# Attention and MLP in one kernel: layer-normed rows transposed by the DMA queue, token rows cast on the way in

## The chip, the cores and the metric

The kernel runs on one core of a Trainium2 chip. The metric is the device time of one execution in microseconds (us), and lower is better. Five engines work side by side, each through its own instructions in order: TensorE (PE in the profile), VectorE (DVE), ScalarE (ACT), GpSimd (POOL) and SyncE (SP, which here only issues transfers). TensorE's weight loads have a row of their own (PEld). They meet at semaphores: an instruction that needs another engine's result, or a landed transfer, waits, and everything behind it on its engine waits with it.

## What is computed

For 8 batches of 8 heads, with 576 tokens and 64 columns a head:

```python
scores = scale * q @ k.T                       # per head, 576 x 576
bias   = -(cum[:, None] - cum[None, :])        # cum = cumsum(max(s, 0))
scores = where(causal, -1e9, scores + minimum(bias, 0))
x      = softmax(scores) @ v                   # heads side by side: 576 x 512 a batch
xn     = (x - mean) / sqrt(var + 1e-6) * g_ln
out    = x + relu(xn @ w_ch1) @ w_ch2          # 512 -> 2048 -> 512
```

Inputs and outputs are float32; the kernel multiplies in bf16.

## The kernel before

**Order.** The order of all instructions is written by hand. A long plan, in words, covers the start (head numbers n up to 17; n counts the 64 heads, batch b = n // 8, head h = n % 8). From n = 18 on, one loop step handles one head. A step first calls `pre(n)`, which issues transfers and casts for later heads; then it puts on TensorE the head's scores, one "unit" of the MLP, on even heads the small last corner of the scores for two heads (`scores_d`), another unit, the product with v of the head two steps earlier (`pv_next`), and some more units.

**Attention of one head.** `scores` multiplies keys and queries into three banks of 512 columns; the bias is four extra rows of the operands (68 rows instead of 64). ScalarE takes the exponential of each bank into `er` (L345). From head 10 on, GpSimd zeroes the masked triangles in `er` with two `affine_select` instructions a head (L354) and one for each two heads (L384). Two steps later `pv` multiplies with v (L412) and `pv_norm` divides on VectorE (L424 to L433). `er` has four slots, used in turn.

**MLP of one batch.** It lies in a queue of 32 units of four matmuls each (128x512): 16 units for the first product (`mlp1`, L520, its relu on ScalarE or VectorE) and 16 for the second (`mlp2`, L538; every fourth ends in `yo`, L547 on VectorE, and an output transfer on SP, L565). The units are spread over eight steps. The queue of batch b-1 is filled at head 3 of batch b, after what was left of the older one has run. The last 64 tokens of two batches are put together into one tile (`xm`, transposed into `xTm`), which is worked off at the very end (`mixed_units`).

**Layer norm.** After the last head of a batch, `pv_next` computes mean and variance and then, one after the other, the 4 (even batches) or 5 (odd batches) tiles `xn` of 128x512 in bf16 on VectorE (L469, L487), and `ln_rstd` (one instruction on VectorE, one on GpSimd, L466). In heads 2 and 3 of the next batch, `ln_tr` transposes each tile on TensorE: four 128x128 transposes into PSUM (L505), and one copy to `xT` or `xTm` by VectorE (ScalarE for batches 1 and 7; L115, L113).

**Keys and queries.** They are needed transposed, with head columns on partitions. Groups `gam` of four heads (two a batch) have one of two homes, `kq0` and `kq1`, in turn. For groups 5 to 15 a group takes this way, for each of five token tiles t: `ld_rows` loads 128 token rows of k and q in float32 (two transfers on SP, L174); `cast_rows` casts them on GpSimd to bf16 (L186) and copies the four bias columns beside them (L187), into one of four row buffers taken in turn; `tr_rows` issues a DMA transpose on SP (L196), which writes the group's home. The row buffers lie in the unused `kq2`. In step n = 4 gam + m the loads are issued at m = -6, -5, -4, the casts at -5, -4, -3 and the transposes at -4, -3, all in `pre(n)`, so ahead of that step's masks on GpSimd.

**Values.** `ld_cast_v` loads v for a batch in five transfers issued by GpSimd that cast on the way (L164): two at 4 steps and three at 3 steps before the batch begins.

**Queues.** SP carries, in program order, the row loads, the row transposes and the outputs; GpSimd's own queue carries v.

Of the kernel before, what the change touches and what calls it, by code (L numbers as in the profile page):

```python
# [15 lines left out]
P = 128  # L16
# [3 lines left out]
def kernel(  # L20
# [11 lines left out]
    nc = tc.nc  # L32
    B, H, S, D = q.shape
# [5 lines left out]
    NF = S // P  # L39
    NT = NF + 1  # L40
    TL = S - NF * P
    SP = NT * P
    BH = B * H
# [4 lines left out]
    NG = BH // G  # L48
    NPE = 5
    NM = 10  # L50
    NR = 4
    KT = 96
    QT = 6
    QP = S // QT
# [34 lines left out]
    def home(gam):  # L89
# [5 lines left out]
        spare[:, i * 2 * G * P : (i + 1) * 2 * G * P].rearrange(  # L95
            "p (u h c) -> p u h c", u=2, h=G
        )
        for i in range(NR)
    ]

    er = const.tile([P, 4, EW], BF16, name="er")
# [9 lines left out]
    def copy_on(eng, out, in_):  # L111
        if eng == "act":
            nc.scalar.copy(out=out, in_=in_)  # L113
        elif eng == "dve":
            nc.vector.tensor_copy(out=out, in_=in_)  # L115
        else:
            nc.gpsimd.tensor_copy(out=out, in_=in_)
# [44 lines left out]
    def ld_cast_v(b, t):  # L162
        pn = P if t < NF else TL
        nc.gpsimd.dma_start(  # L164
            out=v_bf[b % 2][:pn, t, :, 0:D],
            in_=v[b, :, t * P : t * P + pn, :].rearrange("h s d -> s h d"),
        )

    def ld_rows(gam, t):
        pn = P if t < NF else TL  # L170
        b, h0 = gam // 2, (gam % 2) * G
        tmp = stage.tile([P, 2, G, D], F32, name="rowtmp", tag="st")
        for u, src in enumerate((k, q)):
            nc.sync.dma_start(  # L174
                out=tmp[0:pn, u],
                in_=src[b, h0 : h0 + G, t * P : t * P + pn, :].rearrange("h s d -> s h d"),
            )
        loaded["rows", gam, t] = tmp

    turn = [0]  # L180

    def cast_rows(gam, t):
        pn = P if t < NF else TL
        r = rows[turn[0] % NR]
        turn[0] += 1
        nc.gpsimd.tensor_copy(out=r[0:pn, :, :, 0:D], in_=loaded.pop(("rows", gam, t))[0:pn])  # L186
        nc.gpsimd.tensor_copy(  # L187
            out=r[0:pn, :, :, D:KA], in_=cT[0:pn, t, :, gam * G : (gam + 1) * G, :]
        )
        ready["rows", gam, t] = r  # L190

    def tr_rows(gam, t):
        pn = P if t < NF else TL
        r = ready.pop(("rows", gam, t))
        o = t * 2 * G * P
        nc.sync.dma_start_transpose(  # L196
            out=kq[home(gam)]
            .rearrange("p u h s -> p (u h s)")[:, o : o + 2 * G * pn]
            .rearrange("p (h s) -> p h s", s=pn),
            in_=r[0:pn].rearrange("p u h c -> p (u h c)"),  # L200
        )

    w1_r = moe_w_ch1.rearrange("(kd p) dh -> p kd dh", p=P)
# [160 lines left out]
    def scores_d(b, j):  # L364
        u0 = (2 * j) % 4
        pe_mask = b * H + 2 * j < NM
        ed = er[0:TL, u0 : u0 + 2, OD : OD + TL]
        d = ps_t.tile([P, 2, TL], F32, name="sd", tag="tr")
        for u in range(2):
            nc.tensor.matmul(  # L370
                d[:, u, :],
                lhsT=k_cols(b, 2 * j + u, NF),
                rhs=q_cols(b, 2 * j + u, NF * P, S)[0][2],
                start=True,
                stop=not pe_mask,
            )
            if pe_mask:
                nc.tensor.matmul(
                    d[:, u, :], lhsT=ident, rhs=maskT[:, 0:TL], start=False, stop=True
                )  # L380
        nc.scalar.activation(out=ed, in_=d[0:TL], func=ACT.Exp, scale=scale)
        if pe_mask:
            return
        nc.gpsimd.affine_select(  # L384
            out=ed,
            in_=ed,
            compare_op=ALU.is_ge,
            fill=0.0,
            base=0,
            pattern=[[0, 2], [1, TL]],  # L390
            channel_multiplier=-1,
        )
# [78 lines left out]
    def ln_xn(b, t):  # L471
        tiles = x_tiles(b)
        if t >= len(tiles):
            return
        if b == 0:
            nc.vector.tensor_scalar(
                out=mean0[:, t : t + 1],
                in0=sum0[:, t, 0:1],
                scalar1=sum0[:, t, 1:2],
                scalar2=1.0 / Dm,  # L480
                op0=ALU.add,
                op1=ALU.mult,
            )
        else:
            ln_aggr(b, t)
        xn = xnp.tile([P, Dm], BF16, name="xn", tag="xn")
        nc.vector.scalar_tensor_tensor(  # L487
            out=xn,
            in0=tiles[t],
            scalar=mvs[b][:, t, 0:1] if b > 0 else mean0[:, t : t + 1],  # L490
            in1=gb,
            op0=ALU.subtract,
            op1=ALU.mult,
        )
        xns[b, t] = xn
        if b > 0 and t == len(tiles) - 1:
            ln_rstd(b)

    def ln_tr(b, t, eng="dve"):
        if (b, t) not in xns:  # L500
            return
        xn = xns.pop((b, t))
        tr = ps_t.tile([P, KD, P], BF16, name="trx", tag="tr")
        for kd in range(KD):
            nc.tensor.transpose(tr[:, kd, :], xn[:, kd * P : (kd + 1) * P], ident)  # L505
        if eng is None:
            return tr
        if t < NF:
            dst = xTs[b][:, :, t * P : (t + 1) * P]
        else:  # L510
            dst = xTm[:, :, (b // 2) * P : (b // 2 + 1) * P]
        copy_on(eng, dst, tr)

    first_unit = [False]

# [63 lines left out]
    def run_units(n, dve_first=False):  # L579
        for i in range(n):  # L580
            if queue:
                first_unit[0] = dve_first and i == 0
                queue.pop(0)()
# [251 lines left out]
    def pre(n):  # L835
        if n == 14:
            for r in rows:
                nc.gpsimd.memset(r[:, :, :, KA:P], 0.0)
        if n in PAIR_LOADS:
            ld_cast_pair(PAIR_LOADS[n])  # L840
        if n in (11, 12):
            ld_w2(n - 9)
        if n in (8, 9):
            aug(n - 5, nc.sync)
        for gam in range(NPE, NG):
            m = n - 4 * gam
            if m == -6:
                ld_rows(gam, 0), ld_rows(gam, 1)
            elif m == -5:
                cast_rows(gam, 0), cast_rows(gam, 1)  # L850
                ld_rows(gam, 2), ld_rows(gam, 3)
            elif m == -4:
                tr_rows(gam, 0), tr_rows(gam, 1)
                cast_rows(gam, 2), cast_rows(gam, 3)
                ld_rows(gam, 4)
            elif m == -3:
                tr_rows(gam, 2), tr_rows(gam, 3)
                cast_rows(gam, 4)
                tr_rows(gam, 4)
        for nb in range(2, B):  # L860
            for t in {-4: (0, 1), -3: (2, 3, 4)}.get(n - H * nb, ()):
                ld_cast_v(nb, t)

    def pv_next():
        pb, ph_ = pend.pop(0)
        pv(pb, ph_)
        pv_norm(pb, ph_)
        if ph_ in (3, 5, 7):
            ln_stats(pb, ph_ // 2 - 1)
        if ph_ == 7:  # L870
            ln_open(pb)
            for t in range({B - 1: 1}.get(pb, NT)):
                ln_xn(pb, t)


    CUTS = ((0, P), (P, 2 * P), (2 * P, S))
# [44 lines left out]
        "U": lambda: run_units(1, True),  # L921
        "u": lambda: run_units(1),
        "p": lambda n: pre(n),
    }

    PLAN = """
# [13 lines left out]
        B.1.0 V.4.1 B.3.0 A.1 p.10 u n.8 s.10 N.4.1 U Q.q.6 v.9 B.0.0 Q.k.6 E.k.6.0:D E.k.6.1:D  # L940
        U E.q.6.0:A p.11 E.q.6.1:A s.11 n.9 A.0 d.10 u d.12 s.12 B.2.1 U B.3.1 u Q.k.7 B.2.0
        Q.q.7 E.q.7.1:A E.q.7.0:A v.10 p.12 s.13 u E.k.7.0:D n.10 A.2 v.11 A.3 E.k.7.1:D u s.14
        n.11 U d.14 Q.k.8 R p.13 v.12 O U p.14 s.15 p.15 E.k.8.0:D u Q.q.8 u E.q.8.1:A u g.0
        n.12 v.13 E.q.8.0:D E.k.8.1:D U d.16 s.16 u p.16 Q.k.9 n.13 g.1 E.k.9.0:D s.17 v.14 n.14
        u Q.q.9 u v.15 n.15 g.2 l.0 u l.2 E.q.9.1:A E.k.9.1:A l.1 U p.17 E.q.9.0:A
    """
    for word in PLAN.split():
        step, _, eng = word.partition(":")
# [5 lines left out]
    for n in range(2 * H + 2, BH):  # L954
        b, h = n // H, n % H
        pre(n)

        end = next(m for m in (8 * i + 3 for i in range(2, B + 1)) if m >= n)
        nu = -(-len(queue) // (end - n + 1)) - 2
        scores(b, h)  # L960
        run_units(1, True)
        if h % 2 == 0:
            scores_d(b, h // 2)
        run_units(1)
        pv_next()
        pend.append((b, h))
        lt = {2: (0, 1), 3: (2, 3, 4)}.get(h, ()) if b > 1 else ()
        for t in lt:
            ln_tr(b - 1, t, "act" if b == 2 else "dve")
            if t != 1 and t != 4:  # L970
                run_units(1)
                nu -= 1
        if n == 2 * H + 2:
            for t in range(3, NT):
                ln_xn(1, t)
        run_units(nu)
        if b > 1 and h == 3:
            run_units(len(queue))
            queue += batch_units(b - 1)
    pv_next()  # L980
    run_units(3)
    pv_next()
    run_units(4)
    for t in range(NT):
        ln_xn(B - 1, t + 1)
        run_units(1)
        ln_tr(B - 1, t, "act")
    run_units(len(queue))
    queue += batch_units(B - 1)
    queue += mixed_units()  # L990
# [30 lines left out]
```

## Time and profile before

| | |
|---|---|
| median of 3 runs | 360.93 us (360.85 to 361.96) |
| the profiled execution | 360.48 us |
| its span, first to last instruction | 358.4 us |
| busy: PE, DVE, ACT, POOL | 350.8, 200.1, 187.4, 162.1 us |
| DMA transposes of row tiles (SP) | 55 |
| row loads (SP) | 110 |
| transposes of `xn` on TensorE | 144 (36 tiles) |

The profile is of one execution. The page gives busy time by engine, then the span in 40 slices, the chain of work that ended last, and the groups of instructions by source line: number, busy time, mean duration of one, the idle time of the engine just before them and what ended it. Other views answer questions: waits, a window's instructions in order of time, a window's busy time. [...]

### The profile page before, as it was taken

The numbers are of one execution on the slowest core, as the hardware profiler recorded it, in microseconds if no ns is written. First come the engines' busy times: TensorE is split into PE (matmuls) and PEld (weight loads), VectorE is DVE, ScalarE is ACT, GpSimd is POOL, SyncE is SP. The second block draws the span as 40 slices with busy tenths as digits, with TensorE's granted clock in tenths as the row PEclk, the third lists the DMA queues.
The fourth block names the chain that finished last, engine by engine and source line by source line (L and its number), as shares of the span: only waits on it lengthen the run. The fifth ranks groups of instructions, "written<-read, shape, count | busy, mean of one in ns | idle before, by whom it ended". The sixth has DMA issues, their size and how long they took to land.

```text
span 358.4 us, 8434 instructions
## 1 busy us (share of the span) xinstructions
PE 350.8 (98%) x3190; PEld 200.6 (56%) x3190; DVE 200.1 (56%) x540; ACT 187.4 (52%) x363; POOL 162.1 (45%) x343
## 2 busy tenths in 40 slices
PE   7999999999999999999999999999999999999995
PEld 3899666554555555555565555555555554444444
DVE  7788888944385537743584539543855482113111
ACT  4899886577424753377326743575247432501500
POOL 9997579257475544445546554665322010000000
PEclk9999999999999999999999999999999999999999
DMA  9999999989999997699969997999610011011013
GB/s 150 169 184 168 199 196 151 191 198 166 168 172 225 153 164 162 168 180 143 183 166 169 153 196 127 222 145 183 144 60 2 3 59 59 2 59 59 0 33 88
DMA packets 164201, 48.54 MB, mean 135 GB/s; under 512 B 152848, under 2 KB 159552, under 8 KB 164160
## 3 DMA queue, kind: packets, MB, share of 16 engines
q1 hardware_dynamic: 111120, 35.35, 52.0%
q0 software_dynamic: 51600, 11.87, 37.4%
q10 hardware_dynamic: 1440, 0.79, 0.9%
q8 instruction: 25, 0.41, 0.5%
q14 instruction: 16, 0.13, 0.1%
HBM read 37.11 MB, written 9.44 MB: 130 GB/s over the span
## 4 chain that ended last, share of the span: by engine, by line
PE 83%; DVE 6%; DMA 3%; POOL 2%; SPq 2%; issue 1%; ACT 1%; POOLq 0%; DVEq 0%; ACTq 0%
PE ph L520 30%; PE py L538 30%; PE pot L412 6%; DMA rowtmp<-in_q_dram 3%; PE sc L334 3%; PE sb L334 3%; PE sa L334 3%; PE ph L800 2%; SPq L174 2%; DVE xn L487 2%; PE trx L505 2%; PE st L698 2%; PE pot L756 1%; PE trt L676 1%; POOL kq L186 1%
## 5 line engine op out<-in xcount | busy, mean ns | idle before, releaser
L538 PE MATMUL py<-w_bf,hT 128*128 128x512 bf16 (+1 forms) x592 | 136.7, 373 | 0.7 <-DVE yo L547 0.7
L520 PE MATMUL ph<-xT,w_bf 128*128 128x512 bf16 x480 | 114.1, 379 | 0.0
L530 ACT ACTIVATE hT<-ph 128x512 bf16<-128x512 f32 x100 | 59.6, 597 | 64.1 <-PE ph L520 64.1
L538 PEld LDWEIGHTS <-hT 128*128 128x128 bf16 x592 | 53.3, 97 | 49.1 <-issue 1.2
L520 PEld LDWEIGHTS <-w_bf 128*128 128x128 bf16 x544 | 48.6, 97 | 49.9 <-issue 2.9
L186 POOL CAST kq<-rowtmp 128x512 bf16<-128x512 f32 (+1 forms) x55 | 34.0, 618 | 78.1 <-DMA rowtmp<-in_q_dram 56.6
L345 ACT ACTIVATE er<-sa 128x512 bf16<-128x512 f32 x56 | 33.4, 596 | 66.3 <-PE sa L334 43.5
L528 DVE TENSOR_SCALAR hT<-ph 128x512 bf16<-128x512 f32 x36 | 24.9, 692 | 57.9 <-PE ph L520 57.6
L354 POOL TENSOR_SCALAR_AFFINE_SELECT er<-er 128x256 bf16<-128x256 bf16 x108 | 42.9, 423 | 21.2 <-ACT er L345 20.8
L334 PEld LDWEIGHTS <-kq 68*128 68x128 bf16 x412 | 29.9, 97 | 22.0
L412 PEld LDWEIGHTS <-er 128*128 128x128 bf16 x840 | 32.8, 98 | 13.2 <-POOL er L354 1.2
L547 DVE SCALAR_TENSOR_TENSOR yo<-py,rstd,xb 128x512 f32<-128x512 f32 x32 | 24.0, 749 | 24.4 <-PE py L538 18.8
L424 DVE RECIPROCAL rinv<-pot 128x5 f32<-128x5 f32 x56 | 10.7, 192 | 46.6 <-PE pot L412 46.4
L412 PE MATMUL pot<-v_bf,er 128*128 128x65 bf16 x840 | 34.9, 194 | 0.7 <-POOL er L354 0.7
L164 POOL DMA_DIRECT2D v_bf<-in_v_dram x40 | 34.3, 869 | 0.4 <-issue 0.3
L345 ACT ACTIVATE er<-sc 128x512 bf16<-128x512 f32 x56 | 34.3, 613 | 0.0
L345 ACT ACTIVATE er<-sb 128x512 bf16<-128x512 f32 x56 | 33.6, 600 | 0.0
L426 DVE TENSOR_TENSOR xb<-pot,rinv 128x256 f32<-128x256 f32 x56 | 23.8, 424 | 1.9
L487 DVE SCALAR_TENSOR_TENSOR xn<-xb,mv,gb 128x512 bf16<-128x512 f32 x28 | 23.0, 820 | 1.0
L450 DVE BATCH_NORM_STATS2 stats<-xb 128x6 f32<-128x128 f32 (+1 forms) x84 | 21.9, 321 | 0.3
L466 POOL TENSOR_TENSOR rstd<-rstd,mhalf 128x4 f32<-128x4 f32 (+1 forms) x8 | 8.9, 1114 | 29.0 <-DVE rstd L465 29.0
L334 PE MATMUL sc<-kq 68*128 68x256 bf16 (+1 forms) x200 | 21.7, 226 | 0.1
(116 smaller groups left out, 364.1 us busy)
## 6 DMA issues: line engine op xcount, KB each, us to landing
out_dram<-yo SPq DMA_DIRECT2D x32, 256.0 KB
rowtmp<-in_k_dram SPq DMA_DIRECT2D x44, 128.0 KB
rowtmp<-in_q_dram SPq DMA_DIRECT2D x44, 128.0 KB
v_bf<-in_v_dram POOLq DMA_DIRECT2D x32, 128.0 KB, 5.8
w_bf<-in_moe_w_ch_dram POOLq DMA_DIRECT2D x8, 512.0 KB, 9.3
kq<-kq SPq DMA_TRANSPOSE x55
kp<-in_k_dram POOLq DMA_DIRECT2D x6, 144.0 KB, 8.8
qp<-in_q_dram POOLq DMA_DIRECT2D x6, 144.0 KB, 9.0
```

What stands on the lines that cost most here:

```text
L164: nc.gpsimd.dma_start(out=v_bf[b % 2][:pn, t, :, 0:D], in_=v[b, :, t * P : t * P + pn, :].rearrange("h s d -> s h d"),)
L186: nc.gpsimd.tensor_copy(out=r[0:pn, :, :, 0:D], in_=loaded.pop(("rows", gam, t))[0:pn])
L334: nc.tensor.matmul(a[:, c + a0 - q0 : c + a1 - q0], lhsT=k_cols(b, h, kb), rhs=cols, start=True, stop=not (pe_mask and diag),)
L345: nc.scalar.activation(out=e[:, o : o + 512], in_=a, func=ACT.Exp, scale=scale)
L354: nc.gpsimd.affine_select(out=two, in_=two, compare_op=ALU.is_ge, fill=0.0, base=0, pattern=[[0, 2], [1, P]], channel_multiplier=-1,)
L412: nc.tensor.matmul(pot[:, t, :], lhsT=e[:, o : o + P], rhs=vv[:, kb, h, :], start=(kb == 0), stop=(kb == last),)
L487: nc.vector.scalar_tensor_tensor(out=xn, in0=tiles[t], scalar=mvs[b][:, t, 0:1] if b > 0 else mean0[:, t : t + 1], in1=gb, op0=ALU.subtrac ...
L520: nc.tensor.matmul(ph, lhsT=w1_bf[:, kd, fb * P : (fb + 1) * P], rhs=xT[:, kd, :], start=(kd == 0), stop=(kd == KD - 1),)
L528: nc.vector.tensor_scalar_max(out=hT[:, fb, :], in0=ph, scalar1=0.0)
L530: nc.scalar.activation(out=hT[:, fb, :], in_=ph, func=ACT.Relu)
L538: nc.tensor.matmul(py[t], lhsT=hT[:, fb, t * P : (t + 1) * P], rhs=w2_bf[:, fb, c0:c1], start=(fb == 0), stop=(fb == FB - 1),)
L547: nc.vector.scalar_tensor_tensor(out=yo, in0=py[t], scalar=rs, in1=x[:, c0:c1], op0=ALU.mult, op1=ALU.add)
```

## The change

Four things change together.

1. For groups 7 to 15 (the first `NHW = 7` stay), the rows are no longer loaded in float32 by SP and cast by GpSimd. GpSimd issues two transfers a tile that cast on the way, straight into the row buffer, and VectorE copies the four bias columns. There are five row buffers, one for each tile t, instead of four in turn.
2. For groups 5 and 6 the old way stays, but transposes and casts move from `pre(n)` to a new `post(n)`, which stands behind the step's scores and so behind its masks on GpSimd.
3. v is loaded one tile a step, from 6 steps (5 for batch 2) before the batch on.
4. For batches 2 to 7 (those handled beyond `NXD = 2`, and the last), `xn` is transposed by a DMA transpose on SP straight into `xT` or `xTm`; the four transposes on TensorE and the copy go. The tiles of `xn` are no longer computed in a row in `pv_next`, but three in head 1 and two in head 2, each followed by its transpose and a unit. The queue is filled at head 4 instead of head 3 (batches 3 to 7). At the end, two units instead of four run ahead of the first `xn`.

```diff
-    NR = 4
+    NHW = 7
+    NXD = 2
...
+    def ld_cast_rows(gam, t):
+        pn = P if t < NF else TL
+        b, h0 = gam // 2, (gam % 2) * G
+        for u, src in enumerate((k, q)):
+            nc.gpsimd.dma_start(
+                out=rows[t][0:pn, u, :, 0:D],
+                in_=src[b, h0 : h0 + G, t * P : t * P + pn, :].rearrange("h s d -> s h d"),
+            )
...
+    def bias_of_rows(gam, t):
+        pn = P if t < NF else TL
+        nc.vector.tensor_copy(
+            out=rows[t][0:pn, :, :, D:KA], in_=cT[0:pn, t, :, gam * G : (gam + 1) * G, :]
+        )
...
+    def ln_tr_dma(b, t):
+        if (b, t) in xns:
+            nc.sync.dma_start_transpose(out=xT_dst(b, t), in_=xns.pop((b, t)))
...
             m = n - 4 * gam
+            ts_ = {-6: (0, 1), -5: (2, 3), -4: (4,)}.get(m, ())
+            for t in ts_:
+                if gam < NHW:
+                    ld_rows(gam, t)
+                else:
+                    ld_cast_rows(gam, t)
+                    bias_of_rows(gam, t)
+            if gam >= NHW:
+                for t in {-4: (0, 1), -3: (2, 3, 4)}.get(m, ()):
+                    tr_rows(gam, t)
+        for nb in range(2, B):
+            t = n - H * nb + (5 if nb == 2 else 6)
+            if 0 <= t < NT:
+                ld_cast_v(nb, t)
+
+    def post(n):
+        for gam in range(NPE, NHW):
+            m = n - 4 * gam
+            for t in {-4: (0, 1), -3: (2, 3)}.get(m, ()):
+                tr_rows(gam, t)
+            for t in {-5: (0, 1), -4: (2, 3), -3: (4,)}.get(m, ()):
+                cast_rows(gam, t)
+            if m == -3:
                 tr_rows(gam, 4)
-        for nb in range(2, B):
-            for t in {-4: (0, 1), -3: (2, 3, 4)}.get(n - H * nb, ()):
-                ld_cast_v(nb, t)
...
             ln_open(pb)
-            for t in range({B - 1: 1}.get(pb, NT)):
-                ln_xn(pb, t)
...
-        end = next(m for m in (8 * i + 3 for i in range(2, B + 1)) if m >= n)
+        end = next(m for m in [8 * i + (3 if i <= NXD else 4) for i in range(2, B)] + [BH + 3] if m >= n)
...
+        post(n)
         run_units(1)
         pv_next()
...
+        elif h in (1, 2):
+            for t in ((0, 1, 2), (3, 4))[h - 1]:
+                ln_xn(b - 1, t)
+                ln_tr_dma(b - 1, t)
                 run_units(1)
                 nu -= 1
...
-    run_units(4)
+    run_units(2)
     for t in range(NT):
-        ln_xn(B - 1, t + 1)
+        ln_xn(B - 1, t)
+        ln_tr_dma(B - 1, t)
         run_units(1)
-        ln_tr(B - 1, t, "act")
```

More of the change, by code (lines that the diff above doesn't have):

```diff
@@ L97 @@
         )
-        for i in range(NR)
+        for i in range(NT)
     ]
@@ L178, in ld_rows @@
         loaded["rows", gam, t] = tmp
-    turn = [0]
+    def ld_cast_rows(gam, t):
[6 more added lines that the diff above has]
+            )
     def cast_rows(gam, t):
         pn = P if t < NF else TL
-        r = rows[turn[0] % NR]
-        turn[0] += 1
-        nc.gpsimd.tensor_copy(out=r[0:pn, :, :, 0:D], in_=loaded.pop(("rows", gam, t))[0:pn])
         nc.gpsimd.tensor_copy(
-            out=r[0:pn, :, :, D:KA], in_=cT[0:pn, t, :, gam * G : (gam + 1) * G, :]
+            out=rows[t][0:pn, :, :, 0:D], in_=loaded.pop(("rows", gam, t))[0:pn]
         )
-        ready["rows", gam, t] = r
+        nc.gpsimd.tensor_copy(
+            out=rows[t][0:pn, :, :, D:KA], in_=cT[0:pn, t, :, gam * G : (gam + 1) * G, :]
[3 more added lines that the diff above has]
+        nc.vector.tensor_copy(
+            out=rows[t][0:pn, :, :, D:KA], in_=cT[0:pn, t, :, gam * G : (gam + 1) * G, :]
+        )
     def tr_rows(gam, t):
         pn = P if t < NF else TL
-        r = ready.pop(("rows", gam, t))
         o = t * 2 * G * P
@@ L199, in tr_rows @@
             .rearrange("p (h s) -> p h s", s=pn),
-            in_=r[0:pn].rearrange("p u h c -> p (u h c)"),
+            in_=rows[t][0:pn].rearrange("p u h c -> p (u h c)"),
         )
@@ L497, in ln_xn, with xT_dst @@
             ln_rstd(b)
+    def xT_dst(b, t):
+        if t < NF:
+            return xTs[b][:, :, t * P : (t + 1) * P]
+        return xTm[:, :, (b // 2) * P : (b // 2 + 1) * P]
+    def ln_tr_dma(b, t):
+        if (b, t) in xns:
+            nc.sync.dma_start_transpose(out=xT_dst(b, t), in_=xns.pop((b, t)))
     def ln_tr(b, t, eng="dve"):
@@ L507, in ln_tr @@
             return tr
[L508 to L512, printed above, removed]
+        copy_on(eng, xT_dst(b, t), tr)
     first_unit = [False]
@@ L846, in pre @@
             m = n - 4 * gam
[L847 to L858, printed above, removed]
+            ts_ = {-6: (0, 1), -5: (2, 3), -4: (4,)}.get(m, ())
[20 more added lines that the diff above has]
+            if m == -3:
                 tr_rows(gam, 4)
-        for nb in range(2, B):
-            for t in {-4: (0, 1), -3: (2, 3, 4)}.get(n - H * nb, ()):
-                ld_cast_v(nb, t)
     def pv_next():
@@ L923 @@
         "p": lambda n: pre(n),
+        "c": lambda n: post(n),
     }
@@ L942 @@
         Q.q.7 E.q.7.1:A E.q.7.0:A v.10 p.12 s.13 u E.k.7.0:D n.10 A.2 v.11 A.3 E.k.7.1:D u s.14
-        n.11 U d.14 Q.k.8 R p.13 v.12 O U p.14 s.15 p.15 E.k.8.0:D u Q.q.8 u E.q.8.1:A u g.0
-        n.12 v.13 E.q.8.0:D E.k.8.1:D U d.16 s.16 u p.16 Q.k.9 n.13 g.1 E.k.9.0:D s.17 v.14 n.14
-        u Q.q.9 u v.15 n.15 g.2 l.0 u l.2 E.q.9.1:A E.k.9.1:A l.1 U p.17 E.q.9.0:A
+        n.11 U d.14 Q.k.8 R p.13 v.12 O U p.14 s.15 p.15 c.15 E.k.8.0:D u Q.q.8 u E.q.8.1:A u
+        g.0 n.12 v.13 E.q.8.0:D E.k.8.1:D U d.16 s.16 u p.16 c.16 Q.k.9 n.13 g.1 E.k.9.0:D s.17
+        v.14 n.14 u Q.q.9 u v.15 n.15 g.2 l.0 u l.2 E.q.9.1:A E.k.9.1:A l.1 U p.17 c.17
+        E.q.9.0:A
     """
@@ L966 @@
         pend.append((b, h))
[L967 to L970, printed above, removed]
+        if b <= NXD:
+            if n == 2 * H + 2:
+                for t in range(3, NT):
+                    ln_xn(1, t)
+            if b > 2 and h == 1:
+                for t in range(NT):
+                    ln_xn(b - 1, t)
+            for t in {2: (0, 1), 3: (2, 3, 4)}.get(h, ()):
+                ln_tr(b - 1, t, "act" if b == 2 else "dve")
+                if t != 1 and t != 4:
+                    run_units(1)
+                    nu -= 1
+        elif h in (1, 2):
+            for t in ((0, 1, 2), (3, 4))[h - 1]:
+                ln_xn(b - 1, t)
+                ln_tr_dma(b - 1, t)
                 run_units(1)
                 nu -= 1
-        if n == 2 * H + 2:
-            for t in range(3, NT):
-                ln_xn(1, t)
         run_units(nu)
-        if b > 1 and h == 3:
+        if n == end:
             run_units(len(queue))
```

## The prediction

> **What bounds the kernel now.** I read the page's busy rows and slices first, then busy time by window, then TensorE's waits, and only then the chain.
>
> ```profile
> PE 350.8 (98%) x3190; PEld 200.6 (56%) x3190; DVE 200.1 (56%) x540; ACT 187.4 (52%) x363; POOL 162.1 (45%) x343
> ...
> PEclk9999999999999999999999999999999999999999
> DMA  9999999989999997699969997999610011011013
> ```
>
> TensorE is busy 98% of the span at full granted clock, no other engine above 56%. The DMA row is nearly full until slice 28: a second suspect. Since busy matmuls overlap, I checked that they really follow each other closely, in the chain from 280 us on:
>
> ```profile
> 290.07 0.22 PE trx L505 x4
> 290.30 0.86 PE py L538 x4
> 291.16 0.22 PE trx L505 x4
> 291.38 0.86 PE py L538 x4
> ```
>
> Four 512-column matmuls start within 0.86 us, four 128-column transposes within 0.22 us, and the next group begins at once. So TensorE is a full pipe: a transpose costs 0.055 us of it, not the 0.219 us of its duration. The steady part in windows: the first line is one batch, the others the only 10 us windows between 60 and 260 us in which TensorE idled (columns: window, its length, busy PE, PEld, DVE, ACT, POOL with counts, clock, DMA share, GB/s).
>
> ```profile
> 99.20:136.90 37.70, 37.70 (x341) 20.96 (x338) 21.98 (x59) 19.90 (x40) 21.97 (x51) 1.00 1.12 178
> 80.00:90.00 10.00, 9.31 (x79) 4.74 (x76) 4.30 (x12) 7.02 (x14) 7.58 (x15) 1.00 1.41 163
> 140.00:150.00 10.00, 9.78 (x94) 5.78 (x93) 8.80 (x23) 2.71 (x7) 2.20 (x5) 1.00 0.58 140
> 220.00:230.00 10.00, 9.54 (x92) 5.53 (x90) 7.45 (x20) 3.97 (x9) 4.89 (x11) 1.00 0.77 191
> ```
>
> A batch is 8 steps of 4.7 us, without any TensorE gap in the first line. Lost in the middle: 0.69 + 0.22 + 0.46 = 1.37 us. TensorE's own waits name who did it:
>
> ```profile
> PE py L538 <- DVE yo L547: 0.7, 2, 0.5
> PE pot L412 <- POOL er L354: 0.7, 1, 0.7
> ```
>
> The second is the 0.69 us at 89.6 us, and GpSimd in order of time shows why:
>
> ```profile
> 85.94 0.60 POOL L186 CAST kq<-rowtmp 64x512 bf16<-64x512 f32 x1 [2.07 <-DMA rowtmp<-in_q_dram]
> 86.50 0.20 POOL L187 COPY kq<-cT 64x32 bf16<-64x32 bf16 x1
> 86.65 2.48 POOL L164 DMA_DIRECT2D v_bf<-in_v_dram  x3
> 89.11 1.49 POOL L354 TENSOR_SCALAR_AFFINE_SELECT er<-er 128x256 bf16<-128x256 bf16 x4
> ```
>
> A cast waited 2.07 us for its load, three v transfers stood behind it, and four masks behind those. The other two gaps (at 145 and 221 us) lie behind five `xn` tiles in a row on VectorE, with `yo` queued after them. The chain's walk through row loads and casts (60 to 90 us) is therefore mostly a chain that had slack; it cost 0.69 us.
>
> **The change, part by part.** The sum starts from the profiled execution, 360.48 us: 358.4 of span and 2.1 around it. The median of the runs, 360.93, is 0.45 above that.
>
> 1. *Transposes off TensorE.* Batches 2 to 7 have 4+5+4+5+4+5 = 27 tiles, 108 transposes. TensorE's program indeed loses 216 instructions, a weight load and a matmul each. 108 x 0.055 = **5.9 us**, all on the bound. Ends: nothing, if something else sets the pace, and 27 x 0.39 = 10.5 us by the busy time of a group of four. I take 5.9, the spacing. With them go 22 copies on VectorE (0.416 us, 9.2 in all) and 5 on ScalarE (0.585): beside TensorE, worth nothing.
>
> 2. *The same transposes on SP.* No row shows one of an `xn`; the nearest is the row tile's, twice as wide:
>
> ```profile
> L196 SPq DMA_TRANSPOSE kq<-kq x55: 1192/1317/2878, 58.8 to 254.1; - x55
> ```
>
> So 0.66 us (half) to 1.32 (the same) of SP each; I take 1.32, to be safe. 4.5 a batch are at most 5.9 us of SP, while 20 row loads at 0.605 (12.1 us) leave it. Landing: the last row transpose starts at 254.1, its last 256-byte packet ends at 256.5, so 2.4 us. Cover: issued in heads 1 and 2, read from head 5 on, at least two steps, 9.4 us. At the end of the kernel the cover is thinner. From the last `pot` it takes 2.0 us of statistics, 0.75 of a `yo`, 0.93 for the first tile, three more issues of 1.32 while tiles come every 0.93, and 2.4 to land: 10.1 us. TensorE has 14 units of 0.865 = 12.1 us. Cost nothing; without the cover, microsecond for microsecond. Outputs queued behind a transpose that waits for `xn` have three `yo` buffers.
>
> 3. *Rows by GpSimd.* A batch loses 10 casts (0.618) and 10 copies (0.206), 8.2 us, and their waits for loads (15 us in the batch above); it gains 20 transfers. Their issue has no row. Nearest:
>
> ```profile
> L164 POOL DMA_DIRECT2D v_bf<-in_v_dram x20: 705/881/945, 115.5 to 238.3; - x20
> ...
> DMA to landing us min/median/max: 4.0/5.7/7.6
> ```
>
> A row transfer has half of v's pieces; the smallest transfer in the trace, kp, takes 0.64 us. I take 0.75, between 0.64 and 0.95. GpSimd then has 22.0 - 8.2 + 15 = 28.8 us of a 37 us batch (26.6 to 32.8): full, not the bound. The worst stretch is heads 2 and 3: 8 row and 2 v transfers (7.8 us), rstd (1.1) and five masks (2.0), 10.9 us in 9.4. Masks come 1.5 us late there, and `pv` reads them two steps on: hidden. New waits: a transfer into a row buffer, and VectorE's bias copy, wait for the previous group's transpose of the same tile. Behind the one stand the masks, behind the other `pv_norm` and `yo`. The transposes go out two steps earlier (9.4 us) and need three issues and a landing, 6.4 us. Cost nothing; a late one would reach TensorE.
>
> 4. *VectorE* gains 45 bias copies. GpSimd's same copy takes 0.208 us, VectorE's nearest (L241, 8 columns) 0.179: 8.1 to 9.4 us against the 9.2 of part 1. Nothing.
>
> 5. *Order.* Masks ahead of casts, v one a step: the 0.69 us goes. `xn` in threes and twos with units between: a `yo` now waits behind two tiles at most, so 0.22 + 0.46 go too. I take **1.37**; nothing is the other end.
>
> Sum: 360.48 - 5.9 - 1.4 = **353.2 us**.
>
> [...]
>
> **Rivals.**
>
> *The steady state gets new waits (late tiles, masks or rows).* For: parts 2 and 3 put more into two in-order queues, and the DMA row is full. Against: two steps of cover each. A microsecond in each of the five batches 3 to 7 gives 358.2; half of it 355.7.
>
> *TensorE's saving isn't worth its time, another resource setting the pace.* For: only the DMA row. Against: no other engine exceeds 22 us of a 37.7 us batch, and TensorE's gaps are 1.4 us in 200. It gives 359.1 to 360.5, no change.
>
> *Slower: GpSimd's transfers limit each other.* The program gives its transfers eight completion semaphores in turn, so each waits for the landing of the eighth before it. A batch has 25 now (20 rows, 5 v) instead of 5, and the masks stand behind them. 25/8 of a landing must fit into a batch of 37.1 us: it decides from 11.9 us on. For: the longest landing in the trace, early on, when GpSimd's queue was full, is 13.8 us. Then a batch takes 43.1, 6.0 more, over 4.5 batches 27 us: 380. Against: 4.0 to 7.6 us in the middle, and bytes grow little: `xn` adds 4.5 x 128 KB to the 6.7 MB of a batch (178 GB/s), while cast rows are written half as long.
>
> **Chances.** Forecast 0.64 (its own range 351.5 to 354.5, the low end for gaps that the busy rows hide); new waits 0.18; no change 0.05; slower 0.13. The predicted time is the first, 353.2. The range 351.0 to 358.5 takes in the first two, which hold 0.82. About 0.3%, 1.1 us, is what a measurement can tell here: faster by more 0.82, within 0.05, slower 0.13.
>
> **What will show it.** Right: 36 transposes left on L505, TensorE busy near 345 us with gaps under 1 us between 60 and 290; GpSimd busy up from 162 to about 192 us (less 45 x 0.82, plus 90 x 0.75); no wait of `ph` on a transfer. Part 2 is wrong if `ph` waits for `xT` after head 4 or at the end; part 3 if issues take well over 1 us, landings pass 10 us, or `pot` waits for `er`; part 4 if `yo` or `rinv` waits for a row transpose; the whole if TensorE's gaps grow by what its work shrinks.

## The result, and the profile after

The changed kernel takes **363.77 us** (median of 19 runs, 360.82 to 368.2) against 360.93 before (19 runs): a ratio of 1.0061 [1.0034, 1.0088], slower by 0.6%. Medians are of all executions, while ratios leave out the few that ran in a slower state (3 of the 19 here). The profiled execution took 364.1 us, with a span of 362.4. The forecast was 353.2, and its range ended at 358.5.

The busy rows and slices of the page after:

```profile
PE 346.9 (96%) x3082; PEld 195.6 (54%) x3082; DVE 196.3 (54%) x562; ACT 185.4 (51%) x359; POOL 194.9 (54%) x344
...
PEclk9999999999999989999999999999999999999999
DMA  9999999999999995999999999999420033011013
```

TensorE has the 108 matmul records fewer that the change takes away (3190 to 3082), so the work did go. But the span grew by 4.0 us. Two things are new in the slices: in the fifteenth (126.8 to 135.9 us) the granted clock is 0.81, and in the one after it the DMA engines, full before and after, fall to half. The waits of TensorE and of VectorE say what holds them (columns: engine and line that wait, who released them, us in all, times, longest):

```profile
PE ph L537 <- DVE hT L545: 8.9, 7, 3.0
```

```profile
DVE kq L201 <- DMA kq<-kq: 22.8, 14, 3.8
```

L537 is the first linear layer; it waits for its PSUM bank, which the relu on VectorE (L545) frees. L201 is the new copy of the bias columns. It waits for a DMA transpose, that of the previous group, which still reads the same row buffer. VectorE in order of time at the largest gap shows that the two are one thing:

```profile
126.32 0.18 DVE L201 COPY kq<-cT 128x32 bf16<-128x32 bf16 x1 [3.77 <-DMA kq<-kq]
128.55 0.18 DVE L201 COPY kq<-cT 128x32 bf16<-128x32 bf16 x1 [2.05 <-DMA kq<-kq]
128.75 0.69 DVE L545 TENSOR_SCALAR hT<-ph 128x512 bf16<-128x512 f32 x1
```

Two copies of 0.18 us stand still for 3.77 and 2.05 us, and the relu, which has nothing to do with rows, stands behind them. There are only two banks for `ph` (the second layer's `py` uses the same two), so TensorE stops. In windows (columns as in the prediction), the first line is the stretch that before the change was 37.70 us of 37.70:

```profile
99.20:136.90 37.70, 33.87 (x294) 18.38 (x293) 20.64 (x65) 18.59 (x39) 27.35 (x46) 0.95 1.58 165
...
130.00:134.00 4.00, 4.00 (x18) 1.77 (x17) 1.43 (x8) 2.31 (x5) 2.48 (x6) 0.57 1.76 187
```

From 130 to 134 us, just after the gap, the granted clock is 0.57: 18 matmuls where the next four microseconds hold 37. That costs another (1 - 0.57) x 4 = 1.7 us, as an estimate.

So the books of this execution close: the forecast's sum, 353.2, plus 8.9 of waits plus 1.7 of clock is 363.8, against 364.1 measured.

Why is the transpose late? From the start of its issue to the last update of its semaphore (read from the trace, 60 to 260 us; minimum, median, maximum) a row transpose took 2.7, 3.9, 6.8 us before and **2.7, 5.3, 9.4 us** after. The forecast had put 2.4.

The time that a transpose had before its copy's turn came was short as well (read from the trace too). Of the 40 copies of groups 8 to 15, ten waited more than 0.2 us for a transpose, 18.5 us in all. In these ten cases the transpose had begun 5.2 to 7.3 us before VectorE reached the copy, and it landed 7.2 to 9.4 us after it began. At the largest gap the two transposes began at 117.0 and 119.2 us and landed at 126.30 and 128.52; the two copies shown above start 0.02 and 0.03 us later. By the forecast, two steps of 4.7 us less at most two issues ahead, 6.8 to 9.4 us would have been left.

### The profile page after: what moved, and what is told of

It is laid out like the page before. It is cut to its first block, busy times and chain, and to the rows that moved or that the text cites. A ratio compares the mean times of both kernels' runs of the same rounds, so it can differ in the third digit from the quotient of the medians.

```text
span 362.4 us, 8277 instructions
## 1 busy us (share of the span) xinstructions
PE 346.9 (96%) x3082; PEld 195.6 (54%) x3082; DVE 196.3 (54%) x562; ACT 185.4 (51%) x359; POOL 194.9 (54%) x344
## 4 chain that ended last, share of the span: by engine, by line
PE 77%; DMA 15%; DVE 4%; ACT 2%; issue 1%; POOL 0%; DVEq 0%; SPq 0%
PE py L555 33%; PE ph L537 24%; DMA kq<-kq 11%; PE pot L424 5%; DMA w_bf<-in_moe_w_ch_dram 4%; PE sc L346 3%; PE sb L346 2%; PE sa L346 2%; PE ph L817 2%; PE st L715 2%; ACT er L357 1%; PE trt L693 1%; PE pot L773 1%; DVE hT L545 1%; PE trx L526 1%
## 5 line engine op out<-in xcount | busy, mean ns | idle before, releaser
L555 PE MATMUL py<-w_bf,hT 128*128 128x512 bf16 (+1 forms) x592 | 134.3, 373 | 0.1
L537 PE MATMUL ph<-xT,w_bf 128*128 128x512 bf16 x480 | 115.1, 381 | 8.9 <-DVE hT L545 8.9
L537 PEld LDWEIGHTS <-w_bf 128*128 128x128 bf16 x544 | 49.4, 98 | 60.5 <-issue 13.5
L366 POOL TENSOR_SCALAR_AFFINE_SELECT er<-er 128x256 bf16<-128x256 bf16 x108 | 45.2, 441 | 49.2 <-ACT er L357 48.4
L545 DVE TENSOR_SCALAR hT<-ph 128x512 bf16<-128x512 f32 x35 | 24.2, 691 | 41.2 <-PE ph L537 36.2
L346 PEld LDWEIGHTS <-kq 68*128 68x128 bf16 x412 | 30.2, 98 | 22.7 <-issue 1.2
L185 POOL DMA_DIRECT2D kq<-in_k_dram x45 | 33.6, 746 | 12.3 <-DMA kq<-kq 9.1
L424 PEld LDWEIGHTS <-er 128*128 128x128 bf16 x840 | 32.8, 98 | 11.9
L165 POOL DMA_DIRECT2D v_bf<-in_v_dram x40 | 35.3, 887 | 0.2 <-issue 0.2
L185 POOL DMA_DIRECT2D kq<-in_q_dram x45 | 33.2, 738 | 0.3 <-issue 0.3
L201 DVE COPY kq<-cT 128x32 bf16<-128x32 bf16 (+1 forms) x45 | 8.9, 215 | 25.2 <-DMA kq<-kq 22.8
```

The lines of the kernel that those rows point to most:

```text
L165: nc.gpsimd.dma_start(out=v_bf[b % 2][:pn, t, :, 0:D], in_=v[b, :, t * P : t * P + pn, :].rearrange("h s d -> s h d"),)
L185: nc.gpsimd.dma_start(out=rows[t][0:pn, u, :, 0:D], in_=src[b, h0 : h0 + G, t * P : t * P + pn, :].rearrange("h s d -> s h d"),)
L346: nc.tensor.matmul(a[:, c + a0 - q0 : c + a1 - q0], lhsT=k_cols(b, h, kb), rhs=cols, start=True, stop=not (pe_mask and diag),)
L366: nc.gpsimd.affine_select(out=two, in_=two, compare_op=ALU.is_ge, fill=0.0, base=0, pattern=[[0, 2], [1, P]], channel_multiplier=-1,)
L424: nc.tensor.matmul(pot[:, t, :], lhsT=e[:, o : o + P], rhs=vv[:, kb, h, :], start=(kb == 0), stop=(kb == last),)
L537: nc.tensor.matmul(ph, lhsT=w1_bf[:, kd, fb * P : (fb + 1) * P], rhs=xT[:, kd, :], start=(kd == 0), stop=(kd == KD - 1),)
```

## The experiments

Theory at this point (A): the bias copies wait on VectorE for row transposes that land late, and the relu behind them holds TensorE. Rivals: the 27 new transposes on SP slow the row transposes down (B); the faster row transfers of GpSimd do (C). A group that the expectations call the n-th is `gam` = n - 1. All ratios are to the kernel before on the same chip, with 95% intervals.

**Taking the bias copies out of VectorE's way.** Two ways: on GpSimd behind the transfers, or on VectorE but only just ahead of the transposes, one or two heads later.

```diff
 # e1_bias_pool: bias_of_rows
-        nc.vector.tensor_copy(
+        nc.gpsimd.tensor_copy(
 # e2_bias_late: pre(n)
                     ld_cast_rows(gam, t)
-                    bias_of_rows(gam, t)
 ...
                 for t in {-4: (0, 1), -3: (2, 3, 4)}.get(m, ()):
+                    bias_of_rows(gam, t)
                     tr_rows(gam, t)
```

> The changed kernel with one engine exchanged: the bias copies of groups 7 to 15 go from VectorE to GpSimd, behind their transfers. Theory A (VectorE's bias copies wait for the previous group's row transposes, 22.8 us in 14 waits, and the relus behind them hold TensorE, 8.9 us): those waits of ph on hT go, GpSimd's waits for row transposes grow from 9.1 us to some 25, masks have two steps of slack, so 353 to 356 us. Theory B (the DMA queues are overloaded by the transposes of xn, and whoever needs a landed transfer waits): the wait only moves, the masks come late, pot waits for er, and the time stays at 360 to 365.

> The changed kernel with the bias copies still on VectorE, but two steps later (one for the last tile), just ahead of the row transposes that need them. Everything else, and the load on the DMA queues, is the same. Theory A: the previous group's transposes have landed by then (their longest landing was 9.4 us, a step is 4.7), so VectorE's 22.8 us of waits go, TensorE's 8.9 us of gaps and the lowered clock behind the longest of them go too: 353 to 355 us. Theory B: transposes still land at a median of 5.3 us and up to 9.4, something else waits for them, 360 us or more.

e1_bias_pool: 360.62 us, 0.9975 [0.9946, 1.0004]. e2_bias_late: **358.24 us, 0.9928 [0.9905, 0.9951]**, 1.3% below the changed kernel and faster than the kernel before. TensorE's busy row and its waits in e2_bias_late:

```profile
PE 345.0 (97%) x3082; PEld 194.4 (55%) x3082; DVE 196.1 (55%) x562; ACT 185.8 (52%) x359; POOL 194.8 (55%) x344
```

```profile
PE sb L346 <- DMA kq<-kq: 3.2, 3, 1.8
PE py L555 <- DMA w_bf<-in_moe_w_ch_dram: 1.5, 1, 1.5
```

No wait of `ph` for a relu is left: A holds, and the place of 45 small copies was worth 0.0133 of the time, 4.8 us (1.3 either way, the two intervals combined). Both kernels missed the times that A gave them (353 to 356 and 353 to 355). The row transposes are as slow as they were (2.8, 5.1, 9.1 us), and now the scores themselves (L346) wait for them. In e1_bias_pool VectorE's wait is gone too, but its median lies in the range of theory B, 360 to 365; why is left open.

**Undoing one of the two moves.** e3_xn_pe sets `NXD = 8`: the normalised rows of batches 2 to 6 go through TensorE again (22 tiles, 88 transposes; batch 7, at the end of the kernel, is not reached by `NXD` and stays on SP). e4_rows_old sets `NHW = 16`: all rows come by SP and GpSimd's casts.

> The changed kernel with only the transposes of xn undone for batches 2 to 6 (88 back on TensorE, 22 copies back on VectorE, the queue filled at head 3 again; the last batch stays with the DMA). Rows still come by GpSimd's transfers, bias copies still wait on VectorE. Theory A: 4.8 us of transposes are back and most of the waits stay, 362 to 368 us; row transposes land a little sooner, so the waits may fall by up to a half, 360 at the least. Theory B: the DMA queues are relieved, the waits go, 357.5 to 359 us, below the kernel before.

> The changed kernel with only the rows undone: all groups are loaded by SP in float32 and cast by GpSimd, now behind the masks; the transposes of xn stay with the DMA. Theory A: no bias copy on VectorE, so no wait there; GpSimd waits for loads as before, but behind the masks: 353 to 355 us. Theory B: the xn transposes come on top of the same load as in the kernel before, transposes land late, ph waits for xT, 358 us or more.

e3_xn_pe: 366.12 us, 1.0101 [1.0063, 1.0139], in the range of A (362 to 368). The same waits stand there, with no `xn` transpose on SP before the last batch:

```profile
PE ph L537 <- DVE hT L545: 5.7, 4, 2.6
```

```profile
DVE kq L201 <- DMA kq<-kq: 18.6, 10, 3.5
```

The row transposes landed in 2.8, 5.2, 9.7 us. B falls. e4_rows_old: 366.12 us, 1.0173 [1.0133, 1.0212], where A had 353 to 355. A miss: theory B, 358 or more with `ph` waiting for `xT`, was right here. There are no bias copies on VectorE, but GpSimd waits for loads that stand in SP's queue among row transposes, outputs and now `xn` transposes, and TensorE waits for an `xn` transpose itself:

```profile
POOL kq L192 <- DMA rowtmp<-in_q_dram: 45.0, 20, 7.0
```

```profile
PE ph L537 <- DMA xT<-xn: 3.0, 1, 3.0
```

GpSimd's wait alone does not explain it: the kernel before waits 56.6 us for the same loads and loses 0.69 us by it. New here are the casts behind the masks, and the `xn` transposes on SP.

e11_order undoes both and keeps only the order (masks ahead of casts, v one tile a head, buffers by tile).

> Of the change only the order: row transposes and casts after the masks, v's transfers one a head, five row buffers in turn by tile; rows by SyncE's loads and GpSimd's casts in all groups, and the normalised rows on TensorE, as before. By the prediction's fifth part the gaps at 90, 145 and 221 us go: 360.7 - 1.4 = 359.3 us. Rival (what e4_rows_old showed: with the casts behind the masks the transposes come late, and SyncE's queue holds loads that wait): 363 us or more, with waits for row transposes above 3 us.

359.69 us, 0.9952 [0.9933, 0.9971]. The wait just shown is 18.9 us there, and no TensorE wait in the steady part is over 0.5 us. So the casts behind the masks do no harm without the `xn` transposes on SP. As `NXD` is 8 here too, batch 7 is still on SP, which by the spacing is 20 x 0.055 = 1.1 us of the 1.7 gained; the expectation overlooked that. Side by side:

| ratio to before | `xn` of batches 2 to 6 on TensorE | by SP |
|---|---|---|
| rows by SP and GpSimd's casts | 0.9952 (e11_order) | 1.0173 (e4_rows_old) |
| rows by GpSimd's transfers | 1.0101 (e3_xn_pe) | 1.0061 (the change) |

In the order of the change neither move pays alone, and the two together don't either. `xn` on SP needs SP's row loads gone; and the rows by GpSimd bring the bias copies with them.

**What makes the landing long.** e12_no_loads is the changed kernel without the row transfers from `gam` 8 on, so that these transposes read old rows.

```diff
-                    ld_cast_rows(gam, t)
+                    if gam == NHW:
+                        ld_cast_rows(gam, t)
```

> The changed kernel without the row transfers of groups nine to sixteen: the row transposes of these groups read what the eighth group left in the row buffers, so 8 of 11 groups by transposes compute on wrong rows; the bias copies on VectorE, the masks and the 45 row transposes stay as they are. Theory (the casting transfers of GpSimd make the landing of a row transpose long): the landing falls from a median of 5.3 us (up to 9.4) to 3.5 or less, the bias copies' wait from 22.8 to under 8 us, and TensorE's waits at the first linear layer from 8.9 to under 2 us: 355.5 us. Rival (the transposes hold each other up, rows and normalised rows on one queue): the landing stays above 4.5 us, and TensorE still waits 5 us or more there: 361 us or more.

357.72 us, 0.9914 [0.9889, 0.994]. VectorE and TensorE:

```profile
DVE kq L201 <- DMA kq<-kq: 8.5, 9, 2.3
```

```profile
PE ph L537 <- DVE hT L545: 5.0, 2, 3.4
```

The first falls from 22.8 to 8.5, nearly as far as the theory said. The second stays at 5.0, as the rival said, though 3.4 us of it are one gap that ends at 88.2 us, before the first transfer that was left out (it is issued at 100.9 us in the changed kernel). The median landing falls only to 4.6 us, just on the rival's side, and the time lies between the two. So the row transfers are not all of it. More is shown by the 40 row transposes that begin from 105 to 255 us, split by whether one of GpSimd's transfers (rows or v) was in flight at any time of their landing. The last two columns are means over the landings of all 40:

| | median landing, us (number): none in flight | some in flight | GpSimd transfers in flight | other transposes in flight |
|---|---|---|---|---|
| before | 3.3 (20) | 4.8 (20) | 0.7 | 0.8 |
| after | 2.7 (3) | 6.1 (37) | 3.7 | 1.4 |
| e12_no_loads | 3.3 (20) | 6.1 (20) | 0.8 | 1.4 |
| e11_order | 3.3 (20) | 5.0 (20) | 0.7 | 1.2 |
| e9_early8 (below) | 2.8 (1) | 4.2 (39) | 2.1 | 1.4 |

Each kernel shows both values. In the kernel before, the two kinds have equally many other transposes beside them (0.8), so these do not make that difference. The change raised the number of transposes that have company from 20 of 40 to 37. Leaving the row transfers out, with as many other transposes in flight, takes the mean landing of the 40 from 5.8 to 4.6 us, where the kernel before has 4.1. So of the 1.7 us that the change adds, the row transfers are 1.2: C is the larger part. Where e12_no_loads is still slow, it is v that is in flight. How the rest divides between v and the transposes among themselves was not separated.

**Cover for a landing of 5 to 9 us.** Cover is the time that a transfer has before its result is needed. Four kernels stand on top of e2_bias_late. In it the largest gap, 1.8 us at 128 us, lies where two heads are short: filling the queue at head 4 makes one stretch of nine heads, whose units come out as 4, 4, 4, 4, 4, 5, 4, 2, 1, and row transposes are issued by the head.

```diff
 # e5_even
         nu = -(-len(queue) // (end - n + 1)) - 2
+        if 2 * H + 4 <= n <= 3 * H:
+            nu = (1, 1, 2, 2, 1)[n - 2 * H - 4]
 # e7_early, for gam >= NHW
-  loads at m: {-6: (0, 1), -5: (2, 3), -4: (4,)}   transposes at m: {-4: (0, 1), -3: (2, 3, 4)}
+  loads at m: {-7: (0, 1), -6: (2, 3), -5: (4,)}   transposes at m: {-4: range(NT)}
```

> The late bias copies as in e2_bias_late (358.24 us), and besides the units of the nine heads from the fifth of batch 2 to the first of batch 3 dealt 3, 3, 4, 4, 3, 5, 4, 3, 3 where they stood 4, 4, 4, 4, 4, 5, 4, 2, 1. Theory (the cover was cut): in e2_bias_late the largest gap, 1.92 us at 128.2 us, stands where the fourth and first head of that stretch last 2.8 and 2.1 us, so that three row transposes of the ninth group go out 4 to 5 us too late for a landing of 8 us. Two heads longer by 1 and 2 units (0.9 and 1.7 us) then take most of that gap away: TensorE's waits for row transposes fall from 3.2 to about 1.5 us, and the median to 356.5 us. Rival (the landing alone, 8 us under the load of three queues, whatever the lengths of the heads): the gap stays at 1.5 us or more, and the median within 0.5 us of 358.2.

> The late bias copies as in e2_bias_late, and besides the loads of v of batch 2 where the kernel before had them (two at the 13th head, three at the 14th, instead of one at each of heads 12 to 16), so that none stands ahead of the last part of w2 on GpSimd's queue. Theory: the wait for w2 (1.5 us at 61 us in e1_bias_pool and e2_bias_late, 0.3 in e3_xn_pe and e4_rows_old, none before) comes from the v load ahead of it: it is gone, 356.7 us. Rival: it is chance of the run, since the changed kernel with the same order showed none: the median stays within 0.5 us of 358.2.

> The late bias copies as in e2_bias_late, and besides from the eighth group on each row transfer one head earlier and all five row transposes at the first free head (five heads ahead of the next group's end, where three of the five stood a head later). Theory (landing of 5 to 9 us under load, issue 1.3 to 2.9 us, cover short by one head for three of five): with a head (4.6 us) more of cover TensorE no longer waits for a row transpose: its 3.2 us go, 355.0 us. Rival (the queue itself is full: five issues of 1.3 to 2.9 us take longer than a head, and GpSimd's transfers now wait for the transposes that read the same buffer): the waits move to the transposes of the normalised rows or to v, and the median stays at 358 or rises to 360.

> The edits of e5_even, e6_v_order and e7_early together. If each takes its own gap away (1.9 at 128 us and 1.5 at 204 us of rows, 1.6 us at 61 us of w2), 358.2 - 4.6 = 353.6 us, which is what the prediction's sum gave (353.2) with no wait left. If the landing under load is what limits whatever the order, 357 us or more, with TensorE's waits for transfers still above 2 us.

e5_even: 357.2 us, 0.9903 [0.9869, 0.9936]. The gap at 128 us is gone, but one of 1.8 us came at 91 us, where group 6 has lost two units of its cover; the interval overlaps that of e2_bias_late. e6_v_order: 358.62 us, 0.9928 [0.9897, 0.9959]: its wait for w2 is gone, the time is not; the rival was right. e7_early: 359.06 us, 0.9948 [0.9928, 0.9968], in the rival's range too; e8_all: 360.68 us, 0.9992 [0.9964, 1.0021], a clear miss of 353.6. In e7_early no TensorE gap over 0.15 us is left between 110 and 260 us, as the theory wanted, but GpSimd shows what went wrong before that:

```profile
87.77 0.77 POOL L185 DMA_DIRECT2D kq<-in_k_dram  x1 [2.57 <-DMA kq<-kq]
...
92.36 0.64 POOL L192 CAST kq<-rowtmp 64x512 bf16<-64x512 f32 x1
```

The earlier transfers of group 7 wait for a transpose, and the last cast of group 6, which was at 84.0 us in e2_bias_late, stands behind them until 92.4; TensorE waits for its group from 94.9 to 97.3 us. The wait removed on VectorE had been put up again on GpSimd. Hence e9_early8: all row transposes at the first free head from group 7 on, the transfers a head earlier from group 8 on only, and the nine heads dealt 4, 4, 4, 3, 3, 5, 4, 3, 2. e10_early8_pe is the same with `NXD = 8` and without the new deal of the units, to weigh the first part of the forecast in a kernel without waits.

> The late bias copies as in e2_bias_late; the units of the nine heads at the end of batch 2 dealt 4, 4, 4, 3, 3, 5, 4, 3, 2; from the eighth group on all five row transposes at the first free head; from the ninth group on the row transfers one head earlier (e7_early had that from the eighth on, and lost 2.6 us at 97 us in the seventh group, whose casts stand behind those transfers on GpSimd's queue, but only 0.2 us in all after 110 us). Theory (a landing of 5 to 9 us under load that a cover of two to three heads must hold): no gap over 0.5 us after 110 us, and the seventh group's at 91 to 97 us at 1 us or less; e5_even's 357.2 less its 0.7 us at 201 us and less 1 us of 2.0 at 91 us, 355.5 us. Rival (the queues are full, gaps only move): the sum of the waits for row transposes stays above 2 us, and the median above 357.

> e9_early8 with the normalised rows of batches 3 to 7 transposed on TensorE again (the new units' deal is left out, since the ends of the queue lie evenly then). By the prediction's first part (108 transposes at 0.055 us, 5.9 us) it is 5.9 us slower than e9_early8 in a kernel in which TensorE does not wait: 361.4 us where e9_early8 is 355.5, with 3.5 to 6 us more of busy time on TensorE. Rival (the transposes lay in TensorE's idle time or cost less): within 2 us of e9_early8.

e9_early8: **354.98 us, 0.9832 [0.9796, 0.9869]**, the fastest kernel here, 1.7% below the kernel before and 2.3% below the change. Its steady windows, beside 9.31, 9.78 and 9.54 before, and the longest wait on GpSimd:

```profile
80.00:90.00 10.00, 9.89 (x94) 5.54 (x93) 4.63 (x14) 7.23 (x14) 8.48 (x17) 1.00 1.40 182
140.00:150.00 10.00, 9.94 (x86) 5.34 (x85) 5.85 (x18) 4.59 (x10) 6.01 (x10) 1.00 1.27 174
220.00:230.00 10.00, 9.95 (x97) 5.62 (x97) 5.86 (x16) 5.76 (x12) 4.20 (x9) 1.00 1.55 177
```

```profile
POOL kq L185 <- DMA kq<-kq: 17.4, 8, 5.5
```

From 60 to 260 us no TensorE gap over 0.15 us is left, though GpSimd now waits more for transposes (17.4 us against 9.1) and a transpose still lands in 4.5 us (median; 7.9 the longest). With a head more of cover nobody is behind those waits. e10_early8_pe: 359.35 us, 0.9937 [0.9918, 0.9956]. Between the two ratios lie 0.0105, 3.8 us (1.5 either way, the two intervals combined). The expectation counted 108 transposes; `NXD` brings back 88 of them (3170 weight loads where e9_early8 has 3082), 4.8 us by the spacing. Not all of it need be the transposes: e10_early8_pe deals its units in another way, and its profile has a wait of 1.1 us for w2 at 61 us that e9_early8 doesn't have. So the transposes off TensorE do pay when nothing else is late; by how much is known only roughly.

## Why the prediction was wrong, step by step

1. *Transposes off TensorE, 5.9 us.* Right in size: TensorE's busy time went from 350.8 to 345.0 us in e2_bias_late. As time, 3.8 (± 1.5) us lie between e10_early8_pe and e9_early8, where the spacing of 88 transposes gives 4.8.
2. *The same transposes on SP, nothing.* Nearly right. The half-wide `xn` does cost nearly the same issue as a row tile (1.22 us against 1.36):

```profile
L518 SPq DMA_TRANSPOSE xT<-xn x24: 1189/1221/2216, 104.4 to 297.8; - x24
```

   TensorE never waited for `xT` in the changed kernel, at the end neither. That it cost nothing hung on part 3: with the row loads still on SP the same step loses 8 us (e11_order to e4_rows_old, 0.0221 of 361), and there TensorE does wait for `xT`.
3. *Rows by GpSimd.* The issue was right (0.75 us a transfer forecast, 0.746 and 0.738 measured, GpSimd 194.9 us busy where 192 were forecast). **The step that failed is the one after it:** "The transposes go out two steps earlier (9.4 us) and need three issues and a landing, 6.4 us. Cost nothing". It has two faults. First, the landing of 2.4 us was measured on the last row transpose of the kernel, at 254 us, where no transfer of GpSimd's is in flight; in the busy stretch of the same trace the median was 3.9 and the longest 6.8, and the change itself raises it to 5.3 and 9.4. With the medians of the changed kernel, 1.36 us an issue and 5.3 a landing, the same sum is 9.4 us, all of the cover it had counted, and above the median the cover is too short: where copies waited, 7.2 to 9.4 us of landing met 5.2 to 7.3 us that were left. The smaller part of that is the cover (6.8 to 9.4 us by the forecast): issues took up to 4.0 us, and some heads were short. Second, of what stands behind the copy it named `pv_norm` and `yo`, not the relu of the next unit, which two banks tie to TensorE.
4. *45 bias copies, nothing.* Their size was right (8.9 us, 0.215 each). Their wait, 22.8 us, was not counted: it was taken for hidden in part 3. The test the prediction set for itself ("wrong if `yo` or `rinv` waits for a row transpose") looked at the wrong neighbours.
5. *Order, 1.37 us.* Right as far as it was tried: e11_order gains 0.0048, 1.7 us [1.0, 2.4], of which 1.1 is batch 7; the other 0.6 fits the 0.69 us gap at 89.6 us, which is gone. It still computes five `xn` in a row, and keeps two gaps of 0.21 us at 145 and 221 us (0.22 and 0.46 before); in e9_early8 these are gone too.

*The sum.* 353.2 us was the time of a kernel without new waits. e9_early8 comes nearest to it: by its ratio it gains 6.1 us [4.7, 7.4] where the sum had 7.3. Its median is 354.98 us; the profiled execution, 352.75, is the fastest of six. So the terms that were worked out hold within the noise, and the one put at nothing cost 10.6 us (8.9 + 1.7) in the profiled execution of the changed kernel.

*The rivals.* "New waits" was the mechanism in kind, but priced at a microsecond a batch where it was two. "Slower" was put on eight transfers in flight, with landings from 11.9 us on; GpSimd's row transfers landed in 8.1 us at most, so that did not happen. The right rival would have been: a landing above 5.4 us (the cover of 9.4 less three issues of 1.32), priced by every instruction behind the bias copy.

*GpSimd's row transfers* issue in 618 to 817 ns in the changed kernel, whose VectorE is busy 54% of the time, and land in 2.6 to 8.1 us (the row shown is that of k; q's issue in 622 to 802 ns):

```profile
L185 POOL DMA_DIRECT2D kq<-in_k_dram x45: 618/764/817, 85.4 to 247.0; - x45
...
DMA to landing us min/median/max: 2.6/4.7/8.1
```

What is left open: why e1_bias_pool gains so much less than e2_bias_late. How much of e9_early8's gain comes from the deal of the units and how much from the earlier transposes was not separated.

## What to carry to other kernels

Take a transfer's latency from the stretch in which it will run, with its longest value, and ask what the change adds beside it: here the landing of 2.4 us, read at the quiet end of the kernel, stood against a median of 3.9 and a longest of 6.8 us in its busy stretch, and 5.3 and 9.4 after the change. An instruction that waits for a transfer belongs just ahead of the one that needs its result, however cheap it is, because everything behind it on its engine waits too (here a relu, behind two copies of 0.18 us that waited 3.77 and 2.05): follow that list until it meets the engine that bounds. And cover counted in loop steps is only as long as those steps: moving the end of a work queue by one head made two of them half as long.

## What the runs showed of the hardware

- In the five kernels of the table above, a row transpose (a DMA transpose within SBUF) landed later beside transfers of GpSimd's: medians of 2.7 to 3.3 us with none in flight, 4.2 to 6.1 us with some.
- After two gaps TensorE's granted clock halved, after a longer one it did not. In the changed kernel a gap of 3.0 us ended at 129.5 us; from 130 to 134 us the granted clock was 0.57 (0.50 from 130.4 to 133.8), with matmuls up to 427 ns apart instead of 216. In e3_xn_pe a gap of 2.6 us ended at 87.9 us, and the clock was 0.50 from 88.4 to 91.8 us (0.995 over the whole span of 364.5). In e12_no_loads a gap of 3.4 us ended at 88.2 us, and the clock from 88 to 92 us was 1.00. So in these runs the length of the gap alone does not tell whether the clock falls; what else decides it, no run here shows.
